# Which queue stores the attention output: from SyncE's to GpSimd's

## The chip, the cores and the metric

The kernel runs on one NeuronCore of a Trainium2 chip. The metric is the device time of one execution in microseconds (us), from start to end on that core. A core has TensorE (matrix products, 2.4 GHz at full clock and 1.2 GHz at the lower one), VectorE, ScalarE and GpSimd (elementwise work), SyncE (here only issuing transfers), and 16 DMA engines that all the issuing queues share. Each engine works through its own instructions in order and waits on semaphores for the others.

## What is computed

Three layers in a row, in float32. The change lies in the first one and in how its result is written to memory.

```python
def _attn_ref(q, k, v):                 # (4, 8, 576, 64) each
    scores = scale * np.matmul(q, k.transpose(0, 1, 3, 2))
    # heads 0-3: the last 32 positions; heads 4-7: every 32nd position
    masks = np.stack([mask_local if h < H // 2 else mask_strided for h in range(H)], axis=0)
    scores = np.where(masks[None, :, :, :], scores, -1000000000.0)
    scores = scores - np.max(scores, axis=-1, keepdims=True)
    attn = np.exp(scores)
    attn = attn / (np.sum(attn, axis=-1, keepdims=True) + 1e-09)
    return np.matmul(attn, v)

def reference(**kwargs):
    x = attn_out.transpose(0, 2, 1, 3).reshape(B * S, H * D)   # 2304 x 512
    x = _moe_ref(x=x, **moe_kwargs)     # each row through the one expert (of 8) that it chooses
    return _moe2_ref(x=x, **moe2_kwargs)   # 512 -> 2048 -> 512, ELU between
```

## The kernel before

Attention runs first, on 16 pairs of heads: 4 batches, and in each the pairs 2, 0, 3, 1 (`PAIRS`). Pairs 2 and 3 have the strided mask, pairs 0 and 1 the local one. One step `n` of the main loop (L1420 to L1461) works on several pairs at once, so that the engines overlap:

- `emit_S(n)` computes the scores on TensorE, adds the mask and takes the maximum on VectorE, and subtracts it on GpSimd (L1272, on `sm_s` or `sm_l`). `emit_exp(n)` at the step's end takes the exponential on ScalarE.
- `emit_T(n + 1, j)` transposes q and k of the next pair.
- `emit_PT(n - 1)` transposes the probabilities, `emit_PV(n - 1)` multiplies them by v on TensorE and scales the result on VectorE into `x_sb` (L1329 strided, L1357 and L1360 local).
- `emit_X(n - 2)` transposes x for the router, `emit_L` and `emit_lg` make the router's logits.
- At the end of the step `load_pair` (L1112) loads q and k of step n + 3 and `load_v` (L1127 strided, L1132 and L1133 local) loads v of step n + 2, all through SyncE's queue.

The result x of a batch lies in two tiles, `xs0` (local heads) and `xs1` (strided heads). Each has one buffer (`bufs=1`), which the next batch writes anew. When the second pair of a kind is done (`pr % 2`), `emit_PV` puts its stores to `x_dram` on the list `stores`: two for the strided heads (L1337, 288 KB each), three for the local ones (L1364, 512 KB, and L1367 twice, 32 KB each). The step after, behind the exponential, those that were on the list before that step's `emit_PV` (`ready`) are issued on SyncE, ahead of the step's loads (L1455). In the last two steps and behind the loop `emit_X` issues them, on SyncE too (L1374). From `x_dram` GpSimd later gathers rows by expert (L467, tile `xg`); the first gathers start inside the attention loop, for a block whose rows all lie in the first two batches.

Behind attention come the experts (to about 350 us) and the dense layer (to the end), which are mostly a stream of TensorE products.

The order on each engine is the order of the program text; a SyncE or GpSimd queue waits at its head, and what stands behind it waits too. GpSimd's other transfers in this stage are three small loads for the router in step 1 (L1190 to L1192).

Of the kernel before, what the change touches and what calls it, by code (L numbers as in the profile page):

```python
# [26 lines left out]
J = 36  # L27
# [1042 lines left out]
def attention(tc, bg, q, k, v, mod, mbias, wg, x_dram, ident, router, bank):  # L1070
    nc = tc.nc
# [13 lines left out]
    NP = len(pairs)  # L1085
# [119 lines left out]
    def emit_bias():  # L1205
        pm = bank("T", "pm", 128, NT)
        nc.tensor.transpose(pm, mf, ident[0:NT, 0:NT])
        nc.vector.tensor_copy(m1, pm)
        nc.vector.tensor_scalar(m0, m1, -1.0, 1.0, ALU.mult, ALU.add)
        sh = [128, NT, E]  # L1210
        nc.gpsimd.tensor_tensor(bt, m0.unsqueeze(2).to_broadcast(sh), bb[:, 0:1].to_broadcast(sh), ALU.mult)
        nc.gpsimd.tensor_tensor(bias, m1.unsqueeze(2).to_broadcast(sh), bb[:, 1:2].to_broadcast(sh), ALU.mult)
        nc.gpsimd.tensor_tensor(bias, bias, bt, ALU.add)
# [20 lines left out]
    def emit_S(n):  # L1234
        b, pr = pairs[n]
        strided = pr >= 2
        q_sb, k_sb = qt[n % 2], kt[n % 2]
        if strided:
            pss = [bank("S", f"ps_sc{r}", 128, 8, J) for r in range(2)]
            for i in range(8):  # L1240
                h, t, y = i // 4, i // 2 % 2, i % 2
                for x in range(2):
                    at = ((4 * h + 2 * x + t) * 2 + y) * J
                    for r in range(2):
                        ro = slice(D * r, D * r + D)
                        nc.tensor.matmul(pss[r][64 * x:64 * x + 64, i], lhsT=q_sb[ro, at:at + 64],
                                         rhs=k_sb[ro, 32 + at:32 + at + J], start=True, stop=True)
            sm = sm_s.rearrange("p (s k) -> p s k", k=D)[:, :, 0:J]
            masks = [mask_s.unsqueeze(1).to_broadcast([128, 8, J])] * 2
            parts = [(0, 8), (8, 16)]  # L1250
        else:
            parts = [(0, TAIL + 1), (TAIL + 1, 9)]
            pss = [bank("S", f"ps_sl{r}", 128, TAIL + 1, KW) for r in range(2)]
            for s in range(TAIL + 1):
                for x in range(2):
                    for r in range(2):
                        if s == TAIL and r > x:
                            continue
                        blk = 64 * (2 * s + (x if s < TAIL else 0))
                        ro = slice(D * r, D * r + D)  # L1260
                        nc.tensor.matmul(pss[r][64 * x:64 * x + 64, s], lhsT=q_sb[ro, blk:blk + 64],
                                         rhs=k_sb[ro, blk:blk + KW], start=True, stop=True)
            sm = sm_l
            masks = [mask_l[:, i:j] for i, j in parts]
        ns, w = sm.shape[1], sm.shape[2]
        mx = m_p.tile([128, ns], F32, tag="mx", name="mx")
        for ps, mk, (i, j) in zip(pss, masks, parts):
            nc.vector.tensor_tensor(sm[:, i:j], ps[:, 0:j - i], mk, ALU.add)
        if not strided:
            nc.vector.tensor_tensor(sm[64:128, TAIL], pss[1][64:128, TAIL], mask_l[64:128, TAIL], ALU.add)  # L1270
        nc.vector.reduce_max(mx, sm, axis=AX.X)
        nc.gpsimd.tensor_tensor(sm, sm, mx.unsqueeze(2).to_broadcast([128, ns, w]), ALU.subtract)  # L1272
        rss[n] = sm

    def emit_exp(n):
# [27 lines left out]
    xs, stores = {}, []  # L1303
# [3 lines left out]
    def emit_PV(n):  # L1307
# [7 lines left out]
        x_sb = xs[key]  # L1315
        xb = x_dram[b * S:(b + 1) * S]
        if strided:
            pss = [bank("P", "ps_v", 128, 8, D) for w in range(2)]
            for g in range(8):
                h, t, r = g // 4, g // 2 % 2, g % 2  # L1320
# [13 lines left out]
            if pr % 2:  # L1334
                o = xb[:, 4 * D:].rearrange("(q w x t) d -> x q w t d", w=2, x=2, t=4)
                for x in range(2):
                    stores.append(lambda eng, x=x: eng.dma_start(o[x], x_sb[64 * x:64 * x + J].rearrange("q (w t) h d -> q w t (h d)", w=2)))  # L1337
            return
        parts = [(0, TAIL + 1), (TAIL + 1, 9)]
        pss = [bank("P", f"ps_v{r}", 128, j - i, D + 1) for r, (i, j) in enumerate(parts)]  # L1340
# [20 lines left out]
        rss.pop(n)  # L1361
        if pr % 2:
            o = xb[0:512, 0:4 * D].rearrange("(s p) d -> p s d", p=128)
            stores.append(lambda eng: eng.dma_start(o, x_sb[:, 0:16].rearrange("p (s h) d -> p s (h d)", h=4)))  # L1364
            e = xb[512:S, 0:4 * D].rearrange("q (i r d) -> r q i d", r=2, d=D)
            for r in range(2):
                stores.append(lambda eng, r=r: eng.dma_start(e[r], x_sb[64 * r:64 * r + 64, 16:18]))  # L1367

    def emit_X(n):

        b, pr = pairs[n]
        h0 = 2 * (pr % 2)
        x_sb = xs[b, pr // 2]
        while stores and n + 2 >= NP:  # L1374
            stores.pop(0)(nc.sync)
        if pr >= 2:
            for half in range(2):
                ps = bank("P", "ps_x")
                o = ps.rearrange("p (q x t) -> p t x q", x=2, t=4)
# [40 lines left out]
    for n in range(NP):  # L1420
        last = n + 1 == NP
        emit_S(n)
        if n < 3:
            keep_busy(3)
# [7 lines left out]
            emit_T(n + 1, 2)  # L1432
            emit_T(n + 1, 3)
        bg.step()
        ready = len(stores)
        if n >= 1:
            emit_PV(n - 1)
        if n >= 2:
# [13 lines left out]
            emit_wg()  # L1452
        if n == 4:
            emit_bias()
        for _ in range(min(ready, len(stores))):  # L1455
            stores.pop(0)(nc.sync)
        if n + 3 < NP:
            load_pair(*pairs[n + 3])
        if n + 2 < NP:
# [31 lines left out]
```

## Time and profile before

| | us |
|---|---|
| median of 3 runs | 743.94 (741.52 to 745.23) |
| the profiled execution | 743.88 |
| its span, first to last instruction | 742.1 |
| TensorE busy | 714.2 (96%) |
| VectorE busy | 555.6 (75%) |
| ScalarE busy | 417.1 (56%) |
| GpSimd busy | 96.2 (13%) |

A view by stretch gives for each engine its busy time and, in brackets, its instructions; then TensorE's granted clock as a share of full speed, the mean busy share of the DMA engines, and the bytes per second that they moved. In a timeline each row is a start, a duration, engine, line, operation, output and input tiles; in square brackets the idle time just before, with what ended it. "issue" there means that the engine waited for nothing that the profile shows. A row of the waits has the waiting engine and line, the engine or transfer that it waited for, and then the sum in us, the count and the longest. PE is TensorE, DVE VectorE, ACT ScalarE, POOL GpSimd; SPq and POOLq are the queues of SyncE and GpSimd.

### The profile page before, as it was taken

Reading aid. Unit: us, or ns where it says so; the run is one execution under the profiler, and the core shown is the slowest. Engines: PE = TensorE matmul, PEld = TensorE weight load, DVE = VectorE, ACT = ScalarE, POOL = GpSimd, SP = SyncE. Lnnn points to the kernel's source line nnn. Section 1 sums busy time; section 2 is a strip of 40 time slices with the busy share of each in tenths; the row PEclk is TensorE's granted clock in tenths of the full one; section 3 lists DMA queues with packets and bytes.
Section 4 is the critical chain, followed back from the end, with each engine's and each line's share of the span. In section 5 each row is a group of like instructions: output and inputs, shape, how many; then the busy total and the mean of one; then the engine's idle time right before and its main releaser. Section 6 shows DMA issues by size and latency. Waiting matters only on the chain.

```text
span 742.1 us, 14009 instructions
## 1 busy us (share of the span) xinstructions
PE 714.2 (96%) x5298; PEld 629.4 (85%) x5298; DVE 555.6 (75%) x1068; ACT 417.1 (56%) x761; POOL 96.2 (13%) x144
## 2 busy tenths in 40 slices
PE   8799798999999999998999999999999999999995
PEld 5687787778888888988989899999899889899993
DVE  4568757776879978776887776787788898777762
ACT  4477575325445454545565546585556677555642
POOL 4422231122020100000000000022000002200003
PEclk9899889999999999999999999999999999999998
DMA  8788783456585686574766465165533345633302
GB/s 189 156 193 193 168 242 105 133 172 221 169 288 189 212 272 217 194 225 152 277 235 221 156 218 163 60 195 174 166 119 114 113 168 173 198 114 114 114 1 86
DMA packets 85800, 127.37 MB, mean 172 GB/s; under 512 B 20151, under 2 KB 56279, under 8 KB 85728
## 3 DMA queue, kind: packets, MB, share of 16 engines
q1 hardware_dynamic: 77984, 99.63, 44.3%
q0 software_dynamic: 7744, 26.79, 10.9%
q8 instruction: 44, 0.72, 0.4%
q14 instruction: 28, 0.23, 0.1%
HBM read 100.18 MB, written 26.21 MB: 170 GB/s over the span
## 4 chain that ended last, share of the span: by engine, by line
PE 51%; POOL 1%; issue 0%; POOLq 0%; ACT 0%
PE h_ps L719 24%; PE o_ps L810 9%; PE o_ps L809 9%; PE o_ps L808 9%; POOL out_dram L819 1%; POOLq L1487 0%; ACT y_sb L817 0%; POOLq L819 0%
## 5 line engine op out<-in xcount | busy, mean ns | idle before, releaser
L810 PE MATMUL o_ps<-wh,gl 128*128 128x512 f32 x282 | 111.2, 394 | 0.0
L809 PE MATMUL o_ps<-wl,gh 128*128 128x512 f32 x282 | 111.0, 394 | 0.0
L808 PE MATMUL o_ps<-wh,gh 128*128 128x512 f32 x282 | 110.6, 392 | 0.0
L794 ACT CAST gh<-t 128x384 fp32r<-128x384 f32 x94 | 48.3, 514 | 105.0 <-DVE t L746 101.7
L490 DVE TENSOR_TENSOR wl<-wraw,wh 128x1024 fp32r<-128x1024 f32 x56 | 69.0, 1233 | 32.6 <-ACT wh L489 29.7
L719 PE MATMUL h_ps<-xa,wh 128*128 128x384 f32 x320 | 87.3, 337 | 2.0 <-PEq L756 2.0
L745 DVE SCALAR_TENSOR_TENSOR t<-e,t 128x384 f32<-128x384 f32 x96 | 53.5, 557 | 27.8 <-ACT e L740 25.3
L800 DVE TENSOR_TENSOR gl<-t,gh 128x384 fp32r<-128x384 f32 x94 | 52.3, 556 | 18.8 <-ACT gh L794 17.0
L719 PEld LDWEIGHTS h_ps<-xa,wh 128*128 128x128 f32 x320 | 59.2, 188 | 8.4 <-issue 2.3
L719 PE MATMUL h_ps<-xa,wl 128*128 128x384 f32 x192 | 64.6, 336 | 0.0
L810 PEld LDWEIGHTS o_ps<-wh,gl 128*128 128x128 f32 x282 | 52.9, 188 | 12.0
L524 PE MATMUL y_ps<-hh,wh 128*128 128x460 f32 (+1 forms) x160 | 61.5, 384 | 0.0
L870 POOL DMA_DIRECT2D wl<-wl_dram x32 | 17.5, 552 | 336.9 <-PE o_ps L810 198.2
L526 PE MATMUL y_ps<-hh,wl 128*128 128x460 f32 (+1 forms) x160 | 60.1, 376 | 0.0
L525 PE MATMUL y_ps<-hl,wh 128*128 128x460 f32 (+1 forms) x160 | 60.0, 375 | 0.0
L489 ACT CAST wh<-wraw 128x1024 fp32r<-128x1024 f32 x56 | 58.4, 1042 | 0.0
L809 PEld LDWEIGHTS o_ps<-wl,gh 128*128 128x128 f32 x282 | 53.0, 188 | 6.3
L808 PEld LDWEIGHTS o_ps<-wh,gh 128*128 128x128 f32 x282 | 53.0, 188 | 6.2
L147 ACT ACTIVATE conv<-conv 128x512 f32<-128x512 f32 x32 | 21.7, 679 | 59.5 <-DVE conv L159 59.5
L719 PE MATMUL h_ps<-xb,wh 128*128 128x384 f32 x192 | 54.6, 338 | 0.0
L874 ACT CAST wh<-wraw 128x1024 fp32r<-128x1024 f32 x48 | 50.1, 1043 | 0.0
L719 PE MATMUL h_ps<-xc,wh 128*128 128x384 f32 x192 | 49.3, 338 | 0.0
(267 smaller groups left out, 1583.5 us busy)
## 6 DMA issues: line engine op xcount, KB each, us to landing
wraw<-w_f SPq DMA_DIRECT2D x48, 512.0 KB
wraw<-in_moe_w_dram SPq DMA_DIRECT2D x80, 256.0 KB
wl<-wl_dram POOLq DMA_DIRECT2D x32, 512.0 KB, 4.4
conv<-in_moe_w_in_dram SPq DMA_DIRECT2D x16, 512.0 KB
conv<-in_moe_w_out_dram SPq DMA_DIRECT2D x16, 512.0 KB
w_f<-conv SPq DMA_DIRECT2D x32, 256.0 KB
wl_dram<-wl SPq DMA_DIRECT2D x16, 512.0 KB
qn<-in_q_dram SPq DMA_DIRECT2D x16, 288.0 KB
```

Of the source, the lines that this page charges most:

```text
L489: nc.scalar.copy(WH[i], raw)
L490: nc.vector.tensor_tensor(WL[i], raw, WH[i].bitcast(F32), ALU.subtract)
L524: nc.tensor.matmul(ps, lhsT=a, rhs=hh, start=f == 0, stop=False)
L525: nc.tensor.matmul(ps, lhsT=a, rhs=hl, start=False, stop=False)
L526: nc.tensor.matmul(ps, lhsT=b, rhs=hh, start=False, stop=f == NCH - 1)
L719: mm = lambda x, v, f, l: nc.tensor.matmul(ps, lhsT=x, rhs=v, start=f, stop=l, skip_group_check=on)
L745: nc.vector.scalar_tensor_tensor(t, e, 1.0, t, ALU.add, ALU.mult)
L800: nc.vector.tensor_tensor(gl, t, gh.bitcast(F32), ALU.subtract)
L808: nc.tensor.matmul(ps, lhsT=a, rhs=hi, start=first, stop=False)
L809: nc.tensor.matmul(ps, lhsT=a, rhs=lo, start=False, stop=False)
L810: nc.tensor.matmul(ps, lhsT=b, rhs=hi, start=False, stop=last)
L874: nc.scalar.copy(WH[slots(n)[nm]], wts[n, nm])
```

## The change

The list `stores` now holds calls that issue on GpSimd. A new function `store_x` issues all that is on it, and `emit_S` calls it right behind its subtraction on GpSimd; `emit_X` calls it in the last two steps and behind the loop. The step's end no longer issues stores. A store that `emit_PV` of step n put on the list, which SyncE issued at the end of step n + 1, is now issued inside `emit_S` of step n + 1, ahead of it in the program, and on another queue. What SyncE issues in the attention loop is loads alone.

```diff
@@ -1270,6 +1270,7 @@
         nc.vector.reduce_max(mx, sm, axis=AX.X)
         nc.gpsimd.tensor_tensor(sm, sm, mx.unsqueeze(2).to_broadcast([128, ns, w]), ALU.subtract)
+        store_x()
         rss[n] = sm
@@ -1334,7 +1335,7 @@
                 for x in range(2):
-                    stores.append(lambda eng, x=x: eng.dma_start(o[x], x_sb[64 * x:64 * x + J].rearrange("q (w t) h d -> q w t (h d)", w=2)))
+                    stores.append(lambda x=x: nc.gpsimd.dma_start(o[x], x_sb[64 * x:64 * x + J].rearrange("q (w t) h d -> q w t (h d)", w=2)))
@@ -1361,18 +1362,22 @@
-            stores.append(lambda eng: eng.dma_start(o, x_sb[:, 0:16].rearrange("p (s h) d -> p s (h d)", h=4)))
+            stores.append(lambda: nc.gpsimd.dma_start(o, x_sb[:, 0:16].rearrange("p (s h) d -> p s (h d)", h=4)))
             e = xb[512:S, 0:4 * D].rearrange("q (i r d) -> r q i d", r=2, d=D)
             for r in range(2):
-                stores.append(lambda eng, r=r: eng.dma_start(e[r], x_sb[64 * r:64 * r + 64, 16:18]))
+                stores.append(lambda r=r: nc.gpsimd.dma_start(e[r], x_sb[64 * r:64 * r + 64, 16:18]))
+
+    def store_x():
+        while stores:
+            stores.pop(0)()
 
     def emit_X(n):
 ...
-        while stores and n + 2 >= NP:
-            stores.pop(0)(nc.sync)
+        if n + 2 >= NP:
+            store_x()
@@ -1432,7 +1437,6 @@
         bg.step()
-        ready = len(stores)
         if n >= 1:
             emit_PV(n - 1)
@@ -1452,8 +1456,6 @@
             emit_bias()
-        for _ in range(min(ready, len(stores))):
-            stores.pop(0)(nc.sync)
         if n + 3 < NP:
             load_pair(*pairs[n + 3])
```

On SyncE, in steps 4 and 5 (the loads of `qn`, `kn`, `vs` and `vl`, and between them the stores of the first batch):

```order
 L1133 DMA vl_134<-in_v_dram 64x2x64
-L1337 DMA x_dram<-xs 72x4x256 x2
 L1112 DMA qn<-in_q_dram 96x2x384
 L1112 DMA kn<-in_k_dram 96x2x384
 L1127 DMA vs_133<-in_v_dram 36x2x512 x2
-L1364 DMA x_dram<-xs 128x4x256
-L1367 DMA x_dram<-xs 64x2x64 x2
 L1112 DMA qn<-in_q_dram 72x2x512
 L1112 DMA kn<-in_k_dram 72x2x512
```

The five stores leave the queue, and the loads close up.

On GpSimd, in the same steps (`bt` and `bias` belong to the router's bias):

```order
 L1202 TENSOR_TENSOR pick<-pick,ident 128x8 x3
 L1272 TENSOR_TENSOR sm_s<-sm_s,mx 128x16x36
+L1338 DMA x_dram<-xs 72x4x256 x2
 L1211 TENSOR_TENSOR bt<-m_227,bb 128x144
 L1212 TENSOR_TENSOR bias<-m_226,bb 128x144
 L1213 TENSOR_TENSOR bias<-bias,bt 128x144
 L1272 TENSOR_TENSOR sm_l<-sm_l,mx 128x864
+L1365 DMA x_dram<-xs 128x4x256
+L1368 DMA x_dram<-xs 64x2x64 x2
 L1272 TENSOR_TENSOR sm_s<-sm_s,mx 128x16x36
```

The same five stores stand behind the subtractions of steps 4 and 5.

VectorE's order does not change, but what it waits for does. In step 6, where the second batch first writes the local buffer of x, before:

```order
L1351 TENSOR_SCALAR rs<-ps_v_1085 128x5 [waits PE_49]
L1351 TENSOR_SCALAR rs<-ps_v_1086 128x4
L1353 RECIPROCAL rs<-rs 128x9 [waits DVE_49]
L1357 TENSOR_TENSOR xs<-ps_v_1085,rs 128x4x64 [waits DMAHW4_49,DMAHW5_49,DMAHW3_49,DVE_49]
L1357 TENSOR_TENSOR xs<-ps_v_1086,rs 128x4x64
L1360 TENSOR_TENSOR xs<-ps_v_1085,rs 128x64
```

And after:

```order
L1352 TENSOR_SCALAR rs<-ps_v_1085 128x5 [waits PE_49]
L1352 TENSOR_SCALAR rs<-ps_v_1086 128x4
L1354 RECIPROCAL rs<-rs 128x9 [waits DVE_49]
L1358 TENSOR_TENSOR xs<-ps_v_1085,rs 128x4x64 [waits DMASW6_49,DMASW7_49,DMASW5_49,DVE_49]
L1358 TENSOR_TENSOR xs<-ps_v_1086,rs 128x4x64
L1361 TENSOR_TENSOR xs<-ps_v_1085,rs 128x64
```

The first product waits for the three local stores of the batch before, in both kernels; DMAHW are the semaphores of SyncE's transfers, DMASW those of GpSimd's.

## Rows read from the trace of the kernel before

**Rows 1.** Busy time by stretch: engines, TensorE's clock, DMA share, GB/s.
```profile
core 0: us, PE busy (x) PEld busy (x) DVE busy (x) ACT busy (x) POOL busy (x), PEclk, DMA share, GB/s
37.80:132.00 94.20, 85.45 (x1691) 73.05 (x1692) 67.92 (x177) 62.91 (x137) 23.57 (x25) 0.95 0.74 183
132.00:742.00 610.00, 598.99 (x3041) 533.57 (x3039) 469.39 (x850) 335.42 (x585) 56.74 (x71) 1.00 0.51 170
78.00:85.50 7.50, 7.33 (x185) 6.55 (x183) 6.10 (x19) 4.92 (x13) 2.31 (x6) 1.00 1.03 215
85.50:89.40 3.90, 0.05 (x4) 0.02 (x1) 2.75 (x12) 0.00 (x0) 1.32 (x1) 0.77 0.71 144
89.40:95.50 6.10, 5.84 (x92) 5.25 (x93) 3.84 (x14) 4.37 (x8) 1.11 (x2) 0.59 0.35 83
```
**Rows 2.** Waits of TensorE, 15 to 140 us: sum, times, longest.
```profile
PE ps_v L1344 <- issue: 3.9, 1, 3.9
PE ps_v L1325 <- issue: 3.9, 1, 3.9
...
PE ps_tr L1226 <- DMA kn<-in_k_dram: 0.8, 1, 0.8
```
**Rows 3.** Timeline of TensorE at its two stops.
```profile
26.68 0.92 PE L1344 MATMUL ps_v<-vl,pt_l 96*64 96x65 f32 x12 [3.92 <-issue]
...
84.37 1.16 PE L1325 MATMUL ps_v<-vs,pt_s 36*64 36x64 f32 x62
89.38 0.48 PE L1325 MATMUL ps_v<-vs,pt_s 36*64 36x64 f32 x2 [3.85 <-issue]
```
**Rows 4.** Timeline of SyncE's queue: the local stores of the first batch.
```profile
45.06 0.41 SPq L1364 DMA_DIRECT2D x_dram<-xs  x1
45.57 1.80 SPq L1367 DMA_DIRECT2D x_dram<-xs  x2
```
**Rows 5.** Waits of SyncE's queue, 0 to 200 us, at the strided stores.
```profile
SPq L1337 <- DVE sm_s L1268: 13.0, 2, 8.3
```
**Rows 6.** Timeline of GpSimd: transfers of step 1, subtractions of steps 4, 5, 6, 13.
```profile
17.85 0.96 POOL L1190 DMA_DIRECT2D wgf<-in_moe_w_gate_dram  x1
18.82 0.58 POOL L1191 DMA_DIRECT2D mi<-in_moe_modality_id_dram  x1
...
39.98 1.15 POOL L1272 TENSOR_TENSOR sm_s<-sm_s,mx 128x576 f32<-128x576 f32 x1 [2.67 <-PE ps_p L1300]
43.51 0.43 POOL L1211 TENSOR_TENSOR bt<-m,bb 128x144 f32<-128x144 f32 x1 [2.38 <-DVE m L1209]
...
47.03 1.63 POOL L1272 TENSOR_TENSOR sm_l<-sm_l,mx 128x864 f32<-128x864 f32 x1 [2.13 <-PE ps_v L1325]
53.44 1.15 POOL L1272 TENSOR_TENSOR sm_s<-sm_s,mx 128x576 f32<-128x576 f32 x1 [4.77 <-ACT pt_l L1301]
...
104.15 1.64 POOL L1272 TENSOR_TENSOR sm_l<-sm_l,mx 128x864 f32<-128x864 f32 x1
```
**Rows 7.** GpSimd's transfers: tiles, count, KB each, median us from issue to landing.
```profile
xg<-x_dram,idx POOLq DMA_INDIRECT x4, 8.2
wgf<-in_moe_w_gate_dram POOLq DMA_DIRECT2D x1, 16.0 KB, 8.8
wl<-wl_dram POOLq DMA_DIRECT2D x32, 512.0 KB, 4.4
```
**Rows 8.** Timeline of VectorE: first products of x in batches 2 and 4.
```profile
49.08 1.29 DVE L1329 TENSOR_TENSOR xs<-ps_v,rec 128x512 f32<-128x512 f32 x2
...
55.52 0.76 DVE L1357 TENSOR_TENSOR xs<-ps_v,rs 128x256 f32<-128x256 f32 x2
...
57.04 1.12 DVE L1268 TENSOR_TENSOR sm_l<-ps_sl,mask_l 128x480 f32<-128x480 f32 x2 [0.63 <-PE ps_sl L1261]
...
115.25 0.74 DVE L1357 TENSOR_TENSOR xs<-ps_v,rs 128x256 f32<-128x256 f32 x2
```
**Rows 9.** DMA queues, 86 to 90 us: instructions (packets, MB, share).
```profile
q8 instruction: 1, 0.02, 1.8%
```

## The prediction

> **What bounds the kernel now.** I began with the busy time by stretch. From 132 us to the end TensorE is busy 598.99 of 610.00 us; in the attention stretch from 37.8 us (before which no store of x is issued) to 132 us it is busy 85.45 of 94.20 us at a mean clock of 0.95, while the DMA engines are busy 0.74 of the time [rows 1]. The change touches only the attention stretch, and since TensorE is nearly full behind it, a microsecond won or lost there reaches the end. So I then asked what TensorE waits for in this stretch. The only wait for a transfer is 0.8 us, one time, for a load of k, and it lies before 37.8 us; the two long ones, 3.9 us each, have no releaser in the profile ("issue") [rows 2]. The second of these lies in the middle of a group: of 64 records of the product with v, 62 start at 84.37 us and the last two at 89.38 us, without an operand that is new to them [rows 3]. The first ends at 26.68 us [rows 3], before any store of x, and the change cannot touch it. Last I read SyncE's queue, GpSimd's and VectorE's around the stores.
>
> **SyncE without stores.** Twenty stores leave its queue: in each of four batches two strided ones, one of 512 KB and two small ones. Their issue is not free: in the first batch the last three take 0.41 and 1.80 us of SyncE's queue [rows 4], and the queue stands still in front of them, for 13.0 us in two cases [rows 5], with the loads of q, k and v for the steps ahead standing behind. These loads will be issued some microseconds sooner. What that is worth on the path I put at nothing: it would have to shorten a wait of TensorE for a load, and rows 2 show one of 0.8 us before the first store and none after. What is late next for these loads is the release of their buffers by TensorE and ScalarE, which the change leaves alone. From below the term is 0; from above it is the second stop, if loads that come sooner drain the queue before it (a rival, below).
>
> **GpSimd with the stores.** Its rows show plain transfers that it issues: 0.96 us for one of 512 pieces, 0.58 us for one of 18 rows [rows 6]. A strided store (288 pieces) I put between the first two, so a pair takes 1.2 to 1.9 us; the local group takes 0.96 + 2 x 0.58 = 2.1 us. Four batches make 13 to 16 us of GpSimd's time. The cover: the subtraction of step 4 ends at 39.98 + 1.15 = 41.13 us and the next instruction starts at 43.51 us, room 2.4 us against 1.9; that of step 5 ends at 47.03 + 1.63 = 48.66 us and the next subtraction starts at 53.44 us, room 4.8 us against 2.1 [rows 6]. The stores stand behind the subtraction, so the exponential that waits for it is not delayed by its own step's stores. If the cover were gone, the next subtraction would be late, and with it ScalarE's exponential and the transposes of the step after. Without that the term is 0. A wait in front of the stores costs nothing: x was written by VectorE one step earlier.
>
> **The reuse of x's buffers.** This is the new wait to fear. There is one buffer for each of the two kinds of x, so VectorE's first product of the next batch waits until the store of the batch before has landed; the wait stands in both kernels, with the other queue's semaphores now. The old store starts at 45.06 us (the large local one) [rows 4]; the new one follows the subtraction at 48.66 us, 3.6 us later. VectorE overwrites that buffer at 55.52 us [rows 8], so the room is 6.86 us. Of the six such places this is the tightest; the first (strided, 41.13 to 49.08 us) has 7.95 us, the last (local, 104.15 + 1.64 = 105.79 to 115.25 us) 9.46 us [rows 6, 8].
>
> No row shows how long a store takes from GpSimd's queue. The nearest: 8.2 us for the gathers (256 KB each, four in a row, in this same stage), 8.8 us for 16 KB in small pieces beside a full load queue, 4.4 us for 512 KB beside the lighter traffic of the last stage [rows 7]. At 4.4 us nothing waits. I take 8.2 us, since the gathers share queue, stage and load: the first place then waits 8.2 - 7.95 = 0.25 us, the tightest 8.2 - 6.86 = 1.3 us, the last none; the three between I count at the mean of the first two, 0.8 us each. VectorE was idle for 0.63 us right behind the tightest place, before its mask addition at 57.04 us [rows 8], which swallows that much each time. What is left is 1.3 - 0.63 = 0.7 us there and 0.2 us at each of the three between, 1.3 us in all; TensorE runs one step ahead of VectorE and hides part, I take half: 0.6 us goes into the sum.
>
> **Sum.** The profiled execution took 743.88 us (742.1 us span and 1.8 us around it); the median of three runs is 743.94, so the two are one number. 743.88 + 0 (SyncE) + 0 (GpSimd's issue) + 0.6 (reuse) = 744.5 us.
>
> **Rival 1, the second stop goes: faster.** In the 7.5 us before the stop the DMA engines are at 1.03 of their time, in the stop at 0.71, and one transfer of instructions (0.02 MB) falls into 86 to 90 us [rows 1, 9]. I read the stop as TensorE out of instructions, their transfer being late behind the loads; the rows place the two together and do not prove it. SyncE's queue stands still in front of the strided stores [rows 5] and then sends its loads in a bunch; without stores they go out evenly, and the bunch that fills 78 to 85.5 us may be thinner. The price: 3.85 us of stop [rows 3], and behind it 5.84 us of busy TensorE at a mean clock of 0.59 [rows 1], that is (1 - 0.59) x 5.84 = 2.4 us; 6.2 us together, so 743.88 - 6.2 = 737.7 us. Against it: the same bytes have to move through engines that are busy 0.74 of this stretch, and the first stop happens without any store.
> The Trainium skill ("Runtime: NRT & Kernel Launch", Instruction fetch mechanics) says that instructions are fetched ahead in blocks of 16 KiB and that crossing a block's border is mostly hidden. By that this rival would have nothing to win and the sum stands; the stop of 3.85 us without a releaser speaks against "hidden" in this stage.
>
> **Rival 2, the stores land late: slower.** One mechanism, at the reuse of x: if a store lands 8.8 us after the last issue of its group instead of 8.2 us after the first, the first place waits 41.13 + 0.8 + 8.8 - 49.08 = 1.6 us, the tightest 48.66 + 1.54 + 8.8 - 55.52 = 3.5 us, the last 105.79 + 1.54 + 8.8 - 115.25 = 0.9 us; with the three between at the mean of the first two, 2.6 us, that is 13.8 us, less 6 x 0.63 us of VectorE's idle time 10.0 us: 743.88 + 10.0 = 753.9 us at the most, about 749 us if half is hidden by TensorE's lead. It decides from 6.86 + 0.63 = 7.5 us from subtraction to landing at the tightest place. For it: 16 KB took 8.8 us on this queue. Against it: loads that run ahead leave the engines freer when the store starts.
>
> **Rival 3, another stop: slower.** The first stop, 26.68 - 3.92 = 22.76 to 26.68 us [rows 3], stands 5 us behind GpSimd's transfers of 17.85 and 18.82 us [rows 6], which took 8 us and more to land [rows 7]: the load queue and GpSimd's were both busy. With the change both are busy after each group of stores. If that makes instructions late once more, it costs what rival 1 would win, 6.2 us: 750.1 us. Against it: the four gathers, just ahead of the subtraction at 104.15 us, also keep both queues busy, and rows 2 hold no third stop for them.
> The Trainium skill ("DMA: Bandwidth & Descriptors", Queues, rings and completion order) says that each DMA engine takes turns between the queues that have work for it, a packet at a time. By that a third busy queue thins the turns of the instructions' one, which is this rival; and a store in a queue of its own need not stand behind the loads, which would land it sooner and weaken rival 2. No row here tells the two apart.
>
> **How the numbers follow.** The sum (742 to 747 us as its own range) 0.39; rival 1 0.32; rival 2 0.17; rival 3 0.12. Likeliest: 744.5 us. The range must leave out no more than 2 in 10: down to 737 us it takes in nearly all of rival 1, up to 750 us half of rivals 2 and 3. A measurement of this kernel can tell about 0.5%, 3.7 us, from no change: faster by more than that 0.32 (rival 1), slower by more 0.28 (rivals 2 and 3, less 0.01 for landings that cost under 3.7 us), within 0.40.
>
> **What would show it.** In the profile after: SyncE's queue without the waits of rows 5, and its loads of q and k issued sooner; the subtractions still following VectorE's maximum at once (if one waits behind a store, the cover term was wrong); VectorE's first product of x waiting for a GpSimd transfer by no more than 1.3 us (more is rival 2); TensorE's list of waits with two stops (the sum), one (rival 1) or three (rival 3), and the mean clock from 37.8 to 132 us at 0.95, above it or below it to match. The prediction is wrong if the stretch to 132 us changes by more than 4 us either way, or if the time moves behind it.

## The result

The changed kernel takes 732.62 us (median of four runs, 730.87 to 735.71), the kernel before 742.73 us beside it (737.29 to 745.23): a ratio of 0.9888, 95% interval 0.9839 to 0.9938, so 4.6 to 12.0 us faster. The prediction, 744.5 us with a range from 737.0 to 750.0, was wrong: the time lies below the range. Its first rival, at 737.7 us, had the right mechanism for the larger part of the gain and was still 5 us too high.

The profiled execution took 735.71 us with a span of 734.0 us; that of before took 743.88 us with 742.1 us. These two lie 8.2 us apart, the medians 10.1; what follows accounts for the profiled ones. The 8.1 us between the spans divide at the last matmul. These are its rows in the timeline of TensorE, of before first and then of the changed kernel:

```profile
732.73 0.39 PE L810 MATMUL o_ps<-wh,xc 128*128 128x512 f32 x1
```
```profile
728.12 0.39 PE L810 MATMUL o_ps<-wh,xc 128*128 128x512 f32 x1
```

It comes 4.6 us sooner, and the tail, the time from its start to the end of the span, is 9.4 us before and 5.9 us after: 3.5 us more. From the router's last logits to the last matmul both kernels take the same, 597.5 and 597.3 us, so the first share was won in attention and carried on unchanged; the second was won behind all of TensorE's work.

### The profile page after: what moved, and what is told of

It is laid out like the page before. It is cut to its first block, busy times and chain, and to the rows that moved or that the text cites. A ratio compares the mean times of both kernels' runs of the same rounds, so it can differ in the third digit from the quotient of the medians.

```text
span 734.0 us, 14004 instructions
## 1 busy us (share of the span) xinstructions
PE 712.0 (97%) x5298; PEld 627.3 (85%) x5298; DVE 555.1 (76%) x1068; ACT 416.4 (57%) x761; POOL 109.3 (15%) x164
## 4 chain that ended last, share of the span: by engine, by line
PE 51%; POOL 1%; issue 0%; POOLq 0%; ACT 0%
PE h_ps L719 25%; PE o_ps L810 9%; PE o_ps L809 9%; PE o_ps L808 9%; POOL out_dram L819 1%; POOLq L1489 0%; ACT y_sb L817 0%; POOLq L819 0%
```

## The profile after

Line numbers have moved by one to five: L1325 is now L1326, L1329 is L1330, L1337 is L1338, L1344 is L1345, L1357 is L1358, L1364 is L1365, L1367 is L1368. First the busy time by stretch of the changed kernel (columns as in [rows 1]), then TensorE's waits from 15 to 140 us and its timeline where the second stop was:

```profile
37.80:132.00 94.20, 87.58 (x1726) 74.16 (x1727) 69.35 (x180) 64.69 (x141) 37.37 (x45) 0.98 0.66 184
132.00:734.00 602.00, 594.55 (x3005) 530.57 (x3005) 467.52 (x849) 332.88 (x581) 56.12 (x71) 1.00 0.52 171
78.00:85.50 7.50, 7.50 (x191) 6.89 (x189) 6.42 (x21) 4.88 (x13) 2.64 (x6) 1.00 0.69 172
85.50:89.40 3.90, 2.64 (x84) 2.36 (x83) 3.83 (x17) 3.61 (x7) 0.95 (x1) 1.00 0.45 152
89.40:95.50 6.10, 5.61 (x115) 5.13 (x114) 5.10 (x21) 3.68 (x10) 3.81 (x5) 1.00 0.86 242
```
```profile
PE ps_v L1345 <- issue: 3.6, 1, 3.6
...
PE ps_sc L1246 <- issue: 0.8, 1, 0.8
```
```profile
84.00 1.16 PE L1326 MATMUL ps_v<-vs,pt_s 36*64 36x64 f32 x64
85.10 0.66 PE L1392 MATMUL ps_x<-ident,xs 128*128 128x128 f32 x4
```

Against [rows 1 to 3]: the first stop is still there (3.6 us, at 26.7 us), the second is gone. All 64 products with v run in one piece where 62 ran, then 3.85 us of nothing, then two. The DMA engines are at 0.69 of 78 to 85.5 us where they were at 1.03, and the clock of 89.4 to 95.5 us is granted in full where its mean was 0.59.

SyncE's queue shows why the engines are freer. Its timeline from 57 us, in the changed kernel:

```profile
57.58 0.32 SPq L1112 DMA_DIRECT2D qn<-in_q_dram  x1
58.96 0.31 SPq L1112 DMA_DIRECT2D kn<-in_k_dram  x1
60.06 0.72 SPq L1127 DMA_DIRECT2D vs<-in_v_dram  x2
63.01 0.30 SPq L1112 DMA_DIRECT2D qn<-in_q_dram  x1
63.74 0.30 SPq L1112 DMA_DIRECT2D kn<-in_k_dram  x1
```

Before, this load of q at 57.58 us stood behind a strided store and left at 65.47 us, that of k at 66.89 us, and from there to 85.7 us the queue sent loads and local stores with hardly a pause:

```profile
63.09 2.28 SPq L1337 DMA_DIRECT2D x_dram<-xs  x2
65.47 1.33 SPq L1112 DMA_DIRECT2D qn<-in_q_dram  x1
```

Now no store stands in front of the loads, and most of the pauses between them stay.

GpSimd's timeline around the first batch, and its stores from issue to landing (tiles, count, KB each, median us):

```profile
40.05 1.15 POOL L1272 TENSOR_TENSOR sm_s<-sm_s,mx 128x576 f32<-128x576 f32 x1 [2.68 <-PE ps_p L1301]
41.15 1.54 POOL L1338 DMA_DIRECT2D x_dram<-xs  x2
43.47 0.43 POOL L1211 TENSOR_TENSOR bt<-m,bb 128x144 f32<-128x144 f32 x1 [0.78 <-DVE m L1209]
...
46.99 1.63 POOL L1272 TENSOR_TENSOR sm_l<-sm_l,mx 128x864 f32<-128x864 f32 x1 [2.12 <-PE ps_v L1326]
48.57 0.83 POOL L1365 DMA_DIRECT2D x_dram<-xs  x1
49.39 1.23 POOL L1368 DMA_DIRECT2D x_dram<-xs  x2
53.40 1.15 POOL L1272 TENSOR_TENSOR sm_s<-sm_s,mx 128x576 f32<-128x576 f32 x1 [2.77 <-ACT pt_l L1302]
```
```profile
x_dram<-xs POOLq DMA_DIRECT2D x8, 288.0 KB, 5.5
x_dram<-xs POOLq DMA_DIRECT2D x4, 512.0 KB, 4.8
...
x_dram<-xs POOLq DMA_DIRECT2D x8, 32.0 KB, 4.7
```

A strided pair takes 1.54 us of GpSimd and a local group 0.83 + 1.23 = 2.06 us, and no subtraction is late: they start at 46.99 and 53.40 us where [rows 6] has 47.03 and 53.44. Of the six reuses of x's buffers one waits, in VectorE's timeline at batch 4, for the two strided stores issued at 92.97 us; four gathers follow these on the same queue from 94.81 us on:

```profile
100.24 1.29 DVE L1330 TENSOR_TENSOR xs<-ps_v,rec 128x512 f32<-128x512 f32 x2 [1.90 <-DMA x_dram<-xs]
```

## The experiments

A stop is a wait of TensorE without a releaser, as in the prediction. Theory A: SyncE's loads, held behind the stores and then sent in a bunch, fill the DMA engines, and TensorE's instructions arrive late. Against it: the stop is chance (C), or the stores only needed a queue of their own (B). Later runs ask for the last 3.5 us. Every ratio below is to the kernel before, run beside it on the same chip, with its 95% interval.

**The changed kernel once more.** No edit.

> The changed kernel once more, for the spread. Theory A and B alike (the gain is the second stop of TensorE): one stop of 3.5 to 4 us without a releaser, in step 2, none near 85 us; median 731 to 735 us. If the gain was chance (theory C), a second stop near 85 us is back in this profile or the median is within 3 us of the kernel before.

738.81 us, ratio 0.9878 (0.9808 to 0.9948); no stop near 85 us, tail 5.9 us. The time itself missed its 731 to 735 us, but the kernel before took 746.14 us beside it, and the ratio is what compares. The gain repeats, and C is unlikely.

**Shifting TensorE's instructions.** Kernel before, with twenty short products at the start:

```diff
+    def short(n):
+        ps = bank("T", "ps_idle")
+        for _ in range(n):
+            nc.tensor.matmul(ps[:, 0:64], lhsT=idle[:, 0:128], rhs=idle[:, 0:64], start=True, stop=True)
...
+    short(20)
```

> The kernel before with 20 short products (64 columns) added to the warm-up on TensorE, at its start, so that every later instruction of TensorE lies some 40 instructions further on in its stream. If the two stops are TensorE out of instructions, they stand at the border of a fetched block and move back in the program: the first from after 20 of 32 records of the product with v of step 2 to some 20 products earlier (to its start or into the transposes before it), the second from after 62 of 64 records to about 42 of 64. If they are waits for an operand or a buffer that the trace does not name, they stay where they are: 20 of 32 and 62 of 64.

744.17 us (one run). A short stop inside the scores of step 8 shows the shift best; the group in TensorE's timeline, before and then with the twenty products (L1246 is L1252 there):

```profile
60.75 0.84 PE L1246 MATMUL ps_sc<-kt,qt 64*64 64x36 f32 x43
62.18 0.44 PE L1246 MATMUL ps_sc<-kt,qt 64*64 64x36 f32 x17 [0.60 <-issue]
```
```profile
60.83 0.60 PE L1252 MATMUL ps_sc<-kt,qt 64*64 64x36 f32 x23
61.75 0.78 PE L1252 MATMUL ps_sc<-kt,qt 64*64 64x36 f32 x37 [0.31 <-issue]
```

It moved from behind record 43 to behind record 23: by twenty, the number of instructions put in front. The first stop moved as expected too, from behind 20 of 32 records to in front of the first:

```profile
24.98 1.15 PE L1350 MATMUL ps_v<-vl,pt_l 96*64 96x65 f32 x32 [2.04 <-POOL oh L227]
```

The profile names GpSimd's `oh` there, but before, the same product started at 21.95 us, ahead of that instruction at 22.83 us, so it does not wait for it. These stops belong to a place in the instruction stream, not to an operand or to a time. The long one near 85 us did not show in this run although the DMA engines were at 1.05 there: the instruction transfer of that stretch falls into 82 to 83 us in its trace, and into 86 to 87 us before. So the share of the DMA engines alone does not decide; when the instructions come does.

**Holding SyncE again.** The changed kernel, with one-row transfers of x on SyncE at the places where the stores stood; the stores stay on GpSimd:

```diff
+                    if x == 0:
+                        marks.append(lambda: nc.sync.dma_start(scrap[n:n + 1].rearrange("o (g d) -> o g d", d=D), x_sb[0:1, :, 3, :]))
...
+            marks.append(lambda: nc.sync.dma_start(scrap[n:n + 1, 0:D], x_sb[0:1, 17, :]))
...
+        for _ in range(min(ready, len(marks))):
+            marks.pop(0)()
```

> The changed kernel, and at the places in SyncE's queue where the stores stood, one transfer of a single row of the same x (to a place nobody reads), four strided and four local in all: SyncE's queue is held as before, the bytes of the stores stay on GpSimd's queue. Theory A (the loads were held and came in a bunch): the second stop is back, 3.9 us and the low clock behind it, median 738 to 743 us. Theory B (the stores needed a queue of their own): no second stop, median 731 to 735 us.

743.98 us, ratio 0.9948 (0.9910 to 0.9986). The stop is back at the same two records, in TensorE's timeline:

```profile
83.94 1.15 PE L1327 MATMUL ps_v<-vs,pt_s 36*64 36x64 f32 x62
87.57 0.37 PE L1327 MATMUL ps_v<-vs,pt_s 36*64 36x64 f32 x2 [2.47 <-issue]
```

But for eight single rows the bytes were as in the changed kernel, only the wait was put back: this speaks for A and against B. The tail stays at 5.9 us, which is the part of the gain that is left.

**Stores on SyncE behind the loads.** Kernel before, the stores of a step moved behind its loads:

```diff
-        for _ in range(min(ready, len(stores))):
-            stores.pop(0)(nc.sync)
         if n + 3 < NP:
             load_pair(*pairs[n + 3])
         if n + 2 < NP:
             load_v(*pairs[n + 2])
+        for _ in range(min(ready, len(stores))):
+            stores.pop(0)(nc.sync)
```

> The kernel before with the stores still on SyncE, but behind the loads of their step instead of ahead of them: no load of the step is held by a store, the bytes share the loads' queue. Theory A: no second stop, median 731 to 736 us. Theory B: the second stop stays, or another takes its place, median 739 to 745 us.

745.83 us, ratio 1.0008 (0.9965 to 1.0051). The stop near 85 us is gone here too, step 11 to step 12 takes 5.5 us against 9.5 before, and still nothing clear of the noise is won: step 6 to step 7 takes 7.6 us instead of 5.4, where TensorE waits for ScalarE's copies, and the tail is 9.4 us. Of the 4.0 us that step 11 to step 12 gives, step 6 to step 7 leaves 1.8, which is less than this interval can tell. A later place on the same queue takes the stop away without the gain.

**Either part alone.** Kernel before with only the local stores over GpSimd, and with only the strided ones (shown):

```diff
-                    stores.append(lambda eng, x=x: eng.dma_start(o[x], ...
+                    gstores.append(lambda eng, x=x: eng.dma_start(o[x], ...
...
+        while gstores:
+            gstores.pop(0)(nc.gpsimd)
```

> One part of the change alone: the twelve stores of the local pairs go over GpSimd, the eight strided ones stay on SyncE in front of the loads. Theory A (loads held behind the stores and then issued in one bunch starve PE's instruction supply): SyncE still stands from about 57 to 63 us, but not from 61 to 71; the bunch is shorter, the DMA share of 78 to 85.5 us lies between 1.03 (before) and 0.69 (after), and the stop near 85 us is under 3.9 us or gone. Theory C (the stop comes and goes by chance): it is as long as before or gone without any tie to that DMA share. Tail: T1 (count of GpSimd transfers, 85 here) gives some value between or at one of 9.4 and 5.9 us; T2 (any store of x on SyncE) gives 9.4.

> The other part alone: the eight stores of the strided pairs go over GpSimd, the twelve local ones stay on SyncE. Theory A: SyncE stands before the local stores of the second batch from about 61 to 70 us and the loads behind them bunch up to about 85 us, so the DMA share of 78 to 85.5 us is above 0.8 and the stop of 2.5 to 4 us near 85 us stays. Theory C: stop or none, without a tie to the DMA share. Tail: T1 (81 transfers) between or at one of 9.4 and 5.9 us; T2 9.4.

742.74 us, ratio 1.0011 (0.9976 to 1.0047), and 742.60 us, 1.0018 (0.9985 to 1.0051): neither half is worth anything. For the local stores I had expected a shorter stop, and it is longer, 4.44 us; for the strided ones it is 3.89 us. SyncE's timelines say why. With the strided stores still there it stands from 57 to 63 us; with the local ones still there, from 62 to 67 us (second fence); behind either, it sends loads up to 78 us and more without a pause:

```profile
56.58 0.64 SPq L1133 DMA_DIRECT2D vl<-in_v_dram  x1
63.47 2.26 SPq L1339 DMA_DIRECT2D x_dram<-xs  x2
65.83 1.35 SPq L1112 DMA_DIRECT2D qn<-in_q_dram  x1
```
```profile
61.56 0.79 SPq L1127 DMA_DIRECT2D vs<-in_v_dram  x2
67.37 0.40 SPq L1366 DMA_DIRECT2D x_dram<-xs  x1
67.87 3.05 SPq L1369 DMA_DIRECT2D x_dram<-xs  x2
71.01 1.25 SPq L1112 DMA_DIRECT2D qn<-in_q_dram  x1
```

One held wait is enough for the bunch.

**Load without a hold, hold without the load.** The changed kernel with three extra copies of q at step 10 (they leave SyncE's queue at 68.92 us), and the kernel before without the loads of v of three steps:

```diff
+        if n == 10:
+            for i in range(3):
+                nc.sync.dma_start(scrap[i].rearrange("p (h e) -> p h e", h=2), q[i, 0:2].rearrange("h (p a) d -> p h (a d)", a=6))
```
```diff
-        if n + 2 < NP:
+        if n + 2 < NP and n not in (8, 9, 10):
             load_v(*pairs[n + 2])
```

> The changed kernel with three copies of 288 KB each from q to a scratch tensor, issued by SyncE at step 10 (near 76 us) ahead of that step's loads; nothing is held before them. Theory A, in the sharper form that it is the load on the DMA engines that starves PE's instruction supply there: the DMA share of 78 to 85.5 us rises from 0.69 to 0.95 or more and a stop of 2 to 5 us comes back between 83 and 90 us; the time loses 3 to 6 us of the gain. If only the holding of SyncE mattered, no stop comes and the time is that of the changed kernel. The tail stays at 5.9 us.

> The kernel before without the loads of v at steps 8, 9 and 10 (some 0.74 MB of the bunch; the pairs of steps 10 to 12 use the v that is there, so part of the output is of other values); the stores stay on SyncE in front of the loads of q and k. Theory A in its sharper form: DMA share of 78 to 85.5 us falls from 1.03 to 0.6 to 0.8 and the stop near 85 us goes or falls under 1.5 us; attention ends 3 to 5 us earlier. If the hold by itself mattered, the stop stays at 3.9 us. The tail stays at 9.4 us.

With the copies: 743.53 us, ratio 0.9946 (0.9914 to 0.9977), so about half of the gain is lost, with no store on SyncE. I read its profile only up to 90 us, since its step 13 to 14 is a long one (15.0 us; see what stays open). Without the loads of v the whole time says nothing (other values send other amounts of work through the experts), so I read attention alone: step 11 to step 12 takes 5.5 us instead of 9.5. The group in TensorE's timeline, with the copies and then without the loads:

```profile
84.48 1.16 PE L1327 MATMUL ps_v<-vs,pt_s 36*64 36x64 f32 x62
87.28 0.27 PE L1327 MATMUL ps_v<-vs,pt_s 36*64 36x64 f32 x2 [1.65 <-issue]
```
```profile
83.96 1.16 PE L1325 MATMUL ps_v<-vs,pt_s 36*64 36x64 f32 x62
85.61 0.27 PE L1325 MATMUL ps_v<-vs,pt_s 36*64 36x64 f32 x2 [0.49 <-issue]
```

The load brings the stop back with SyncE free, and without it the stop nearly goes with SyncE still held at 63 us. So the hold is only the way to the bunch, and the bunch is what makes the stop. Seven of the kernels, with the microsecond in which the instruction transfer falls (the queue named "instruction" in one-microsecond stretches of the DMA view):

| kernel | DMA share 78 to 85.5 us | instruction transfer in | last two records at | stop |
|---|---|---|---|---|
| changed | 0.69 | 81 to 82 | in one piece with the 62 | none |
| before, fewer loads of v | 0.62 | 82 to 83 | 85.61 | 0.49 |
| changed, with copies | 1.04 | 84 to 85 | 87.28 | 1.65 |
| changed, SyncE held | 0.92 | 85 to 86 | 87.57 | 2.47 |
| before | 1.03 | 86 to 87 | 89.38 | 3.85 |
| strided stores alone | 0.94 | 86 to 87 | 89.12 | 3.89 |
| local stores alone | 0.98 | 87 to 88 | 90.58 | 4.44 |

The share orders them only roughly (0.98 stops longer than 1.04); the transfer's time orders these seven. Five more kernels, which come below, stop at the same two records: twenty small transfers (3.03 us), twelve of 128 rows (1.66), the same with rows apart (4.13), twelve of 512 pieces (3.58), six of those (3.31). With them the time alone no longer orders the stops, since TensorE reaches the place at other times: with rows apart the transfer starts at 83.80 us, sooner than the 86.61 us of before, and the stop is longer. What holds for all eleven kernels that stop there is that the two records start 2.5 to 2.9 us after the transfer's first packet. In the seven profiles without a stop there, the one with twenty short products among them, TensorE comes to these records 3.0 us or more behind it and has no need to stop.

**Two buffers for the strided x.** The changed kernel with

```diff
-            xs[key] = xs_p.tile(sh, F32, tag=f"xs{pr // 2}", name="xs")
+            xs[key] = xs_p.tile(sh, F32, tag=f"xs{pr // 2}", bufs=2 if strided else 1, name="xs")
```

> The changed kernel with two buffers for the strided x instead of one, so that the multiplication of the fourth batch need not wait for the store of the third. If the reuse wait of 1.9 us near 100 us costs what the sum of the prediction gave it, the wait is gone and the time is 0 to 2 us under the changed kernel (about 731 to 738 beside a kernel before of 742 to 746); if it lies beside other work, the time is that of the changed kernel. No long stop near 85 us, tail 5.9 us in either case.

733.08 us, ratio 0.9911 (0.9879 to 0.9943). The wait of 1.9 us is gone, and the time is that of the changed kernel. In the changed kernel step 14 to 15 takes 9.0 us and the last logits come 20.7 us after it; here it is 8.0 and 21.7, the same sum. The reuse term is worth nothing.

**The first stop.** The changed kernel with the router's transfers of GpSimd one step later, and with the loads of v of two early steps one step later:

```diff
         if n == 1:
-            load_router()
             router.constants()
+        if n == 2:
+            load_router()
```
```diff
+        if n in (2, 3):
+            load_v(*pairs[n + 1])
-        if n + 2 < NP:
+        if n + 2 < NP and n not in (1, 2):
```

> The changed kernel with the three router transfers of GpSimd (small rows, landing in 8 to 9 us) issued one step later, at step 2 instead of step 1. If these are the load that starves the supply at the first stop (3.4 to 3.9 us near 27 us in both kernels), that stop goes or halves and the time is 2 to 4 us under the changed kernel; if the loads of q, k and v do it (DMA share 0.97 from 20 to 26.7 us, of which SyncE's loads are the most), it stays as it is and the time with it. Tail 5.9 us.

> The changed kernel with the loads of v for the fourth and fifth pair issued one step later (steps 2 and 3 instead of 1 and 2); nothing else moves. Theory A: the DMA share of 20 to 26.7 us falls under the 0.97 of both kernels, the first stop (3.4 to 3.9 us near 27 us) shrinks to under 2 us, and the time is 1 to 4 us under the changed kernel, unless the same bytes starve a later stretch; then the stop moves there and the time stays within 1 us of the changed kernel (ratio to before 0.986 to 0.991). If DMA load is not the cause, the first stop stays at 3.4 to 3.9 us. Tail 5.9 us.

739.50 us, ratio 0.9911 (0.9881 to 0.9941), with a first stop of 2.55 us; and 733.95 us, 0.9915 (0.9886 to 0.9944), with 2.72 us. The kernel with two buffers, whose early steps are untouched, has 2.7 us as well, so neither edit shortened it beyond its own scatter. In both the DMA share of 20 to 26.7 us is still 0.96. Moving two loads of v by one step does not thin this stretch, which is full on both sides of it too (0.91 from 14 to 38 us in the changed kernel, 0.96 with the loads moved); whether a thinner one would end this stop was not tried. No version beat the changed kernel.

**The end: twenty small transfers.** Kernel before, stores on SyncE, with small GpSimd transfers behind the subtractions:

```diff
+    def send_small():
+        while small:
+            small.pop()
+            nc.gpsimd.dma_start(scrap[len(seen)], ident[0:16, :])
+            seen.append(1)
```

> The kernel before, with twenty small GpSimd transfers (16 rows of 512 B of a constant, to a scratch tensor) added where the changed kernel has its twenty stores; the stores themselves stay on SyncE. It separates two readings of the 9.4 us (before) and 5.9 us (after) between the last matmul and the end. Theory T1 (the number of transfers that GpSimd issued sets how long its last DRAIN takes): DRAIN falls from 7.46 us to about 3.8, the tail is 5.9 us, and the time is 3 to 4 us under the kernel before. Theory T2 (the stores' bytes, or SyncE's own stores, set it): DRAIN stays at about 7.46 us and the tail at 9.4. In both the long stop of PE near 84 to 89 us stays, since SyncE is held by the stores as before; if it goes, the theory that held loads cause it is in trouble.

743.31 us, ratio 1.0025 (0.9995 to 1.0054), and the tail is 11.3 us: the count does matter, but the other way. In all these kernels the last thing is the wait for GpSimd's queue to empty, a DRAIN. Its row at the launch's line has least, median and greatest duration of three in ns, and the first and last start. Before, changed, and with twenty small transfers:

```profile
L1487 POOLq DRAIN  x3: 51/109/7464, 733.8 to 741.8; - x3
```
```profile
L1489 POOLq DRAIN  x3: 46/109/3813, 729.2 to 733.7; - x3
```
```profile
L1499 POOLq DRAIN  x3: 46/109/9112, 732.7 to 742.7; - x3
```

Twenty more transfers cost 9.11 - 7.46 = 1.65 us, 0.082 us each. The halves of the change fit that line (8 more: 8.13 us; 12 more: 8.45 us), the changed kernel, with 20 more, does not. GpSimd's timeline shows what it has instead, some 45 us before the end:

```profile
670.58 1.06 POOL L870 DMA_DIRECT2D wl<-wl_dram  x2 [14.63 <-PE o_ps L809]
686.34 0.53 POOL L870 DMA_DIRECT2D wl<-wl_dram  x1 [14.71 <-PE o_ps L809]
688.77 0.55 POOL L870 DMA_DIRECT2D wl<-wl_dram  x1 [1.90 <-issue]
```

The last pair of wl loads is split by 1.90 us with no releaser, where every earlier pair runs on. The six profiled kernels of this study that also have all stores on GpSimd show the same 1.90 us there and a DRAIN of 3.81 to 3.83 us; no kernel with stores on SyncE shows that gap between its wl loads. I read the gap as GpSimd clearing finished transfers early, beside busy engines, so that its last DRAIN has fewer to go through; no row names what it does there.

**What sets the clearing off.** Four kernels, each the one before with added GpSimd transfers, the stores still on SyncE: twelve of 128 rows; twelve whose rows lie apart in the target; twelve of 512 pieces of 128 B; six of those.

```diff
+            nc.gpsimd.dma_start(scrap[len(seen)], ident)
```
```diff
+            nc.gpsimd.dma_start(scrap[len(seen)][:, 0:128], ident)
```
```diff
+            nc.gpsimd.dma_start(scrap[len(seen)].rearrange("p (c e) -> p c e", c=4)[:, :, 0:32], ident.rearrange("p (c e) -> p c e", c=4))
```

> The kernel before, its stores on SyncE, with twelve GpSimd transfers of 128 rows of 512 B of a constant to a scratch tensor, three per batch. They bring GpSimd's queue to 85 transfers (as in e8_local, whose last DRAIN was 8.45 us) and to the 9472 packets of the changed kernel (e8_local has 8576). Theory T3 (once the queue has been given more packets than some bound between 8640 and 9472, GpSimd clears finished transfers in the middle, before the last wl load, and its last DRAIN has fewer to go through): a gap of 1.9 us splits the last pair of wl loads near 690 us, DRAIN is under 4.5 us, the tail 5.9 to 6.5 us instead of 9.4, and the kernel is about 3 us under the one before. Theory T1 (count alone): DRAIN 8.45 us, tail 10.4. Theory T2 (stores of x on SyncE): no gap, tail 9.4 or more. The stop near 85 us stays by all of them.

> The kernel before, stores on SyncE, with twelve GpSimd transfers of 128 rows of 512 B as in e10_full12, but to rows that lie apart in the scratch tensor, so that each row is a packet of its own (144 packets each by the count of the local stores, 9472 in all, as in the changed kernel; 85 transfers). Theory T3 (the queue's packets set off a clearing in the middle): a gap of 1.9 us splits the last pair of wl loads, DRAIN falls to 3 to 4.5 us, the tail from 9.4 to about 6, and the kernel is 3 to 4 us under the one before. Theory T1 (count of transfers alone): no gap, DRAIN 8.45 us, tail 10.4. Theory T2 (SyncE's own stores, or the bytes of x, set it): as T1 here.

> The kernel before, stores on SyncE, with twelve GpSimd transfers that each send 512 pieces of 128 B of a constant to a scratch tensor (6144 pieces; 85 transfers in all). Theory T4 (the number of contiguous pieces in GpSimd's queue sets off the clearing, at a bound that 3072 extra pieces don't reach and 5376 do): a gap of 1.9 us splits a pair of wl loads near 690 us or earlier, the last DRAIN falls from 7.46 us to about 3.8, the tail from 9.4 to about 6, and the kernel is 2 to 4 us under the one before, with the stop near 85 us still there. Theory T2 (it needs that SyncE has no stores of x): no gap, DRAIN 8.45 us, tail 10.4.

> As e17_chunks12, with six of these transfers (3072 pieces, as many as the local stores alone have; 79 transfers). T4 with a bound on the pieces: no gap, DRAIN 7.95 us by 0.082 us for each of six transfers, tail 9.9. If small pieces as such set it off: a gap here too and a DRAIN under 5 us. T2: as T4.

The first two missed their aim: the trace counts 8128 packets on the queue in both, not 9472. Extra pieces below are worked out from the shapes of the added transfers (a piece is what lies contiguous on both sides):

| kernel | GpSimd transfers | extra pieces | gap of 1.9 us | last DRAIN, us | last matmul to end, us | ratio |
|---|---|---|---|---|---|---|
| before | 73 | 0 | no | 7.46 | 9.4 | 1 |
| six of 512 pieces | 79 | 3072 | no | 8.00 | 9.9 | one run, 747.96 us |
| strided stores alone | 81 | 2304 | no | 8.13 | 10.0 | 1.0018 |
| local stores alone | 85 | 3072 | no | 8.45 | 10.4 | 1.0011 |
| twelve of 128 rows | 85 | 1536 | no | 8.48 | 10.4 | 1.0017 (0.9991 to 1.0042) |
| twelve, rows apart | 85 | 1536 | no | 8.46 | 10.4 | 1.0013 (0.9987 to 1.0040) |
| twelve of 512 pieces | 85 | 6144 | not there | 4.84 | 7.0 | 0.9975 (0.9944 to 1.0005) |
| twenty small | 93 | 320 | no | 9.11 | 11.3 | 1.0025 |
| changed | 93 | 5376 | yes | 3.81 | 5.9 | 0.9888 |

With 6144 extra pieces, and stores still on SyncE, DRAIN falls from the line's 8.45 to 4.84 us and the tail to 7.0 us, while TensorE's stop near 85 us stays (3.58 us). So it is what GpSimd has to describe, not SyncE's being free of stores, that sets the clearing off, at a bound above 3072 and at or below 5376 extra pieces. The packets don't (8128 in all three rows of twelve, of which one clears), nor does the count, nor do the bytes (27.57 MB on the queue here, 29.15 MB with either part of the change alone). Against what I expected there is no gap between the wl loads of this kernel. Its trace shows another place: the ScalarE copy that the first of the last six scatters of the output waits for ends at 732.15 + 0.59 = 732.74 us, and GpSimd starts that scatter 1.36 us later. In all seventeen other profiles it follows 0.28 us behind the copy:

```profile
732.15 0.59 ACT L818 COPY y_sb<-o_ps 128x512 f32<-128x512 f32 x1 [0.30 <-PE o_ps L811]
```
```profile
734.10 1.02 POOL L820 DMA_INDIRECT out_dram<-y_sb,idxd  x1 [36.85 <-ACT xc L795]
```

So GpSimd was held 1.08 us there by something that the profile does not show, and that is the difference between this tail and the changed kernel's; from the end of the last scatter's issue to the end both take 3.4 us, the kernel before 6.9. That it clears its queue in this place fits, and is not shown.

## Why the prediction was wrong, point by point

- **SyncE without stores, put at nothing: this step failed.** I priced loads that leave sooner only by TensorE's waits for a load, and there was one of 0.8 us. Their worth lay in what their bunch does to another queue. What the runs showed in its place is a stop of 3.85 us that goes when the loads come spread out. Rival 1 named exactly that, and I gave it a chance of 0.32; the evidence for it was in [rows 1, 3, 9], and I let "the same bytes have to move" and the first stop outweigh it. The one-row transfers, with which the stop came back at the same bytes, show that the spacing of the bytes counts, and the copies and the left-out loads that their number does. The first stop was no argument against it: its stretch (20 to 26.7 us) is at 0.97 before any store.
- **Rival 1's price.** 6.2 us was too much for the stop: from step 11 to step 12 the kernel before takes 9.5 us and the changed one 4.7, so 4.8 us, and 4.6 us arrive at the last matmul. The term that was mis-sized is the slow clock: of the 2.4 us I gave it, the trace bears out about 4.8 - 3.85 = 1.0 us (four transposes behind the stop take 1.11 us before, at 89.78 us, and 0.66 us after; the step that follows takes 7.5 us before and 7.8 after, so the rest of the slow stretch cost nothing).
- **The end of the kernel was not in the sum at all.** It assumed that a gain in attention is the whole gain. 3.5 us of the 8.1 lie in GpSimd's last DRAIN, which no rival had; that rival 1's 6.2 us lie as near to 8.1 as they do is luck, a price too high for the stop beside a term left out. The prediction did say that it is wrong "if the time moves behind it"; it had no term for a queue whose end costs by what went through it.
- **GpSimd's issue, at nothing: right.** 1.54 and 2.06 us against 1.2 to 1.9 and 2.1; every subtraction shown on time.
- **Reuse of x, 0.6 us: wrong place, no harm.** The stores land in 4.7 to 5.5 us in the median, not 8.2, so the place I called tightest does not wait; the one that does is batch 4's strided one, with the gathers right behind its stores, by 1.9 us, and the run with two buffers shows that it costs nothing in the end. Rival 2 falls with this.
- **Rival 3, another stop: did not come** in the profile of the changed kernel. The signs named for rival 1 did: one stop, a mean clock of 0.98 to 132 us instead of 0.95, and the last logits 4.4 us sooner.

The Trainium skill ("Runtime: NRT & Kernel Launch", Instruction fetch mechanics) says that crossing a block's border is mostly hidden. The runs agree where the DMA engines have room (none in the changed kernel near 85 us) and disagree where they have none (3.85 us before): by the rule rival 1 would have had nothing to win, and the stop in the trace already spoke against it.

What stays open: with twenty products put in front, the instruction transfer follows the one ahead of it by 8.2 us, as before (8.3 us), but that one comes at 74.0 us instead of 78.3 us, and why is not shown. A step 13 to 14 of 13.4 to 15.0 us instead of 7.7, with short stops at 95 to 105 us, stands in ten of the eighteen profiles, of the changed kernel and of kernels with the stores on SyncE alike. These ten are all the profiles of three groups of kernels run beside each other, in which the kernel before takes 745.8 to 746.5 us; the three other groups, where it takes 740.2 to 742.7 us, have none. So this step goes with the group and not with the queue of the stores, each ratio is taken within a group, and the cause of the step is open.

## What to carry to other kernels

A wait of TensorE without a releaser, at one fixed record of a group and with the DMA engines full ahead of it, is a reason to spread transfers out, even where no engine waits for data. A store that waits on a queue in front of loads does more than delay them: it turns them into a bunch, and half of the holds removed may be worth nothing while the last one makes the bunch alone. Follow the last matmul and the end of the span apart, since a change of queue can move the time between them.

## What the runs showed of the hardware that was not expected

- GpSimd's last DRAIN grows by 0.082 us with each transfer that the kernel gave its queue (73, 79, 81, 85 and 93 transfers: 7.46, 8.00, 8.13, 8.45 and 9.11 us), and with 93 transfers it takes 3.8 us where a gap of 1.9 us, which no engine waited for, stands between two issues ahead of it.
- A transfer of 0.02 MB of instructions comes 4 us after the one before it where the DMA engines are at 0.64 (77 to 81 us), and 8 us after it where they are at 1.02 (78 to 86 us). In eleven kernels TensorE stands at one place of its instructions, for 0.5 to 4.4 us, and goes on 2.5 to 2.9 us after the transfer's first packet.
- Stores of 288 and 512 KB on GpSimd's queue land in 5.5 and 4.8 us in this stage, where the gathers took 8.2 us before [rows 7] and take 6.3 us in the changed kernel.
